# Where scores, value products and transposes stand in PE's order: slots 5 to 17 and the first batch of an attention and bilinear FFN kernel

## The chip, the cores and the metric

One core of a Trainium2 chip. Times are device microseconds of one execution. The profile's span starts a little later and ends a little earlier: an execution of 415.64 us has a span of 413.9.

## The reference

```python
scores = scale * q @ k.T                      # 8 batches, 8 heads, 576 x 576, head size 64
scores += bias_table[bucket(|i - j|)]         # relative position bias
attn = softmax(scores)                        # without a mask
x = (attn @ v) -> (4608, 512)                 # heads side by side
out = ((x @ w_a) * (x @ w_b)) @ w_out         # 512 -> 1536 -> 512
```

## The kernel before

Two heads make a pair; the 32 pairs are worked on in 32 slots. In slot s, PE computes the scores of pair s and the value products of pair s - 1, and the FFN's matmuls of finished batches fill the rest. ACT takes exponentials from PSUM, DVE multiplies by exp(bias) (`mul`) and normalises (`norm`). 576 is 4 x 128 + 64, so each pair has "tail" scores and a 64-column corner, `qktt`.

```python
def qk_tail(p):                               # tail scores of pair p
    ps = ps_sc.tile(...)
    ...
    pt = bank(AV if wide(p) else TR, FP32, f"qktt{p}")     # the corner's own bank
    ...
def ex_tail(p):                               # ACT: L395 reads the corner, then L397 or L400 the rest
```

PSUM has two banks for FFN units (FF, used in turn) and one each called AV and TR. AV holds value products 0 to 2 of a pair, TR products 3 and 4, and both also take transposes, corner scores and, in `run`, one FFN unit each. `run(s, four)` interleaves the four score tiles of slots from 9 on with four half-row FFN units; between two halves a 1x1 copy on DVE (`hop`) must have run. After it:

```python
first = o[0:1] or rest[0:1]                   # an output unit, or, where the plan has none, an input unit
rest = rest if o else rest[1:]
steps += [lambda: run(s, four), lambda: qk_tail(s), lambda: put_in(first, FF), lambda: ex_tail(s),
          lambda: mul(s, 0)] + TQ + X(o[1:2]) + [lambda: mul(s, 1)]
steps += TK + X(o[2:]) if o else []
steps += [A(0, 1, 2), N(0)]                   # value products 0 to 2, norm
steps += [] if o else TK
steps += X(rest[0:1]) + [lambda: mul(s, 2), A(3, 4), N(3), lambda: t_x(s - 1), lambda: turns(s)]
...
```

`TQ` and `TK` are PE's transposes of the next pair's queries and keys with their copies (slots up to 10); `t_x` and `turns` issue transposing DMAs from the SP queue: the attention output of the pair before, and from batch 3 on the queries, keys and tails of the next batch.

The softmax here doesn't subtract the row's maximum and nothing guards it: scores larger than these inputs give would overflow.

## Time and profile before

| | before |
|---|---|
| time, median of 4 | 414.91 us (414.62 to 414.97) |
| PE busy share, DVE, ACT | 96%, 49%, 59% |
| slot 11 and slot 17, score start to score start | 8.30 and 9.16 us |
| a usual slot (19 to 30) | 10.79 us |

PE is the bound almost everywhere, so a slot's length, read from the timeline as the start of one slot's first score matmul to that of the next, shows at once what a wait costs. The prediction shows the lines that matter (its list of PE's waits is a choice: the page also has 1.2 us before the first scores and a few of 0.2 to 0.7 us).

### The profile page before, as it was taken

To read this page: it belongs to the slowest core of one execution; us is meant where nothing else is said; L and a number is where in the kernel's file an instruction comes from. 1 tells how busy PE (TensorE), PEld (TensorE's weight loads), DVE (VectorE), ACT (ScalarE), POOL (GpSimd) and SP (SyncE) were. 2 spreads that over 40 slices of the span, in tenths; PEclk is the share of its full clock that TensorE was granted. 3 is DMA by queue.
4 is the path that set the end of the run, shared out by engine and by line. 5 is a ranking of instruction groups with operands and counts; after the bars stand their busy time and mean duration, and the time that the engine had idled before them with its cause. 6 is when DMAs were issued, how large, how long until landed. Compare 5 with 4: busy or idle time off the path is not lost.

```text
span 413.9 us, 9454 instructions
## 1 busy us (share of the span) xinstructions
PE 399.2 (96%) x3831; PEld 218.9 (53%) x3890; DVE 201.0 (49%) x531; ACT 244.0 (59%) x345; POOL 119.6 (29%) x161
## 2 busy tenths in 40 slices
PE   8799999999999999999999999999999999999996
PEld 3574555566656555555555555555555544444443
DVE  4685666656465444644455455555544330430330
ACT  4997476676887666766666666666666222322321
POOL 9897848904455006600550030000000000000000
PEclk9999999999999999999999999999999999999999
DMA  9999999999979939992899249421111202002004
GB/s 159 189 155 178 158 159 150 180 147 125 140 54 169 164 47 85 152 143 63 78 170 145 64 61 122 92 65 42 35 35 41 65 2 102 2 0 102 2 1 101
DMA packets 164940, 40.83 MB, mean 99 GB/s; under 512 B 155320, under 2 KB 160224, under 8 KB 164896
## 3 DMA queue, kind: packets, MB, share of 16 engines
q0 software_dynamic: 110448, 18.75, 63.9%
q1 hardware_dynamic: 53168, 21.03, 27.7%
q8 instruction: 30, 0.49, 0.5%
q10 hardware_dynamic: 1280, 0.43, 0.5%
q14 instruction: 14, 0.11, 0.1%
HBM read 38.77 MB, written 9.45 MB: 116 GB/s over the span
## 4 chain that ended last, share of the span: by engine, by line
PE 82%; DMA 10%; POOL 4%; issue 2%; DVE 1%; ACT 1%; POOLq 0%; DVEq 0%
PE pa L538 21%; PE po L538 21%; PE pb L538 20%; PE av L432 7%; PE qk L347 6%; DMA wb<-in_moe_w_b_dram 4%; DMA kn<-in_k_dram 4%; PE av L423 2%; DMA vm<-in_v_dram 2%; PE qkt L378 2%; PE qkt L375 1%; PE po L555 1%; POOL qn L134 1%; POOL kn L134 1%; DVE XG L469 1%
## 5 line engine op out<-in xcount | busy, mean ns | idle before, releaser
L538 PE MATMUL pb<-xn,wb 64*128 64x512 bf16 (+1 forms) x592 | 156.6, 377 | 1.3
L538 PE MATMUL pa<-xn,wa 128*128 128x512 bf16 (+1 forms) x609 | 157.2, 377 | 0.7 <-DVE XG L469 0.3
L358 ACT ACTIVATE at<-qk 128x1024 bf16<-128x1024 f32 x128 | 129.3, 1026 | 38.6 <-PE qk L347 36.3
L544 ACT ACTIVATE ha<-pa 128x512 f32<-128x512 f32 x108 | 64.8, 600 | 61.8 <-PE pa L538 60.7
L538 PEld LDWEIGHTS <-wa 64*128 64x128 bf16 (+1 forms) x616 | 56.6, 96 | 44.3 <-DVE XG L469 2.3
L538 PEld LDWEIGHTS <-wb 64*128 64x128 bf16 (+1 forms) x616 | 56.8, 96 | 41.1 <-issue 1.5
L548 DVE TENSOR_TENSOR g<-pb,ha 128x512 bf16<-128x512 f32 x60 | 41.5, 692 | 65.5 <-PE pb L538 38.3
L366 DVE TENSOR_TENSOR at<-at,W 128x512 bf16<-128x512 bf16 (+1 forms) x128 | 59.4, 483 | 2.3 <-DMA W<-bias_tab 2.1
L128 POOL DMA_DIRECT2D vm<-in_v_dram x32 | 28.2, 918 | 95.1 <-PE av L432 83.5
L573 ACT ACTIVATE ob<-po 128x512 f32<-128x512 f32 x35 | 20.9, 598 | 55.6 <-PE po L538 53.6
L538 PE MATMUL po<-wo,g 128*128 128x512 bf16 x216 | 51.8, 379 | 0.6
L432 PEld LDWEIGHTS <-at 128*128 128x128 bf16 x992 | 39.3, 97 | 8.7 <-issue 3.3
L432 PE MATMUL av<-vm,at 128*128 128x65 bf16 x992 | 42.9, 193 | 0.0
L548 DVE TENSOR_TENSOR q<-pb,ha 128x512 bf16<-128x512 f32 x32 | 22.1, 692 | 41.8 <-ACT ha L544 21.0
L423 PE MATMUL av<-vt,att 128*128 128x130 bf16 x156 | 34.6, 222 | 2.3 <-ACT att L395 2.2
L538 PEld LDWEIGHTS <-g 128*128 128x128 bf16 x228 | 21.5, 98 | 22.9 <-issue 0.7
L468 DVE RECIPROCAL rc<-av 128x6 f32<-128x6 f32 x64 | 12.1, 188 | 44.1 <-PE av L432 43.5
L469 DVE TENSOR_TENSOR XG<-av,rc 128x384 bf16<-128x384 f32 x64 | 31.4, 491 | 2.2
L347 PE MATMUL qk<-QTb,KTb 64*128 64x512 bf16 x160 | 32.0, 379 | 0.0
L128 POOL DMA_DIRECT2D qn<-in_q_dram x28 | 24.3, 911 | 21.7 <-PE trq L296 14.3
L538 PE MATMUL po<-wo,q 128*128 128x512 bf16 x116 | 29.6, 379 | 0.6
L128 POOL DMA_DIRECT2D kn<-in_k_dram x28 | 24.4, 914 | 3.4 <-DMA wb<-in_moe_w_b_dram 1.8
(133 smaller groups left out, 349.2 us busy)
## 6 DMA issues: line engine op xcount, KB each, us to landing
out_dram<-ob SPq DMA_DIRECT2D x32, 256.0 KB, 2.3
vm<-in_v_dram POOLq DMA_DIRECT2D x28, 128.0 KB, 5.5
qn<-in_q_dram POOLq DMA_DIRECT2D x24, 128.0 KB, 8.0
kn<-in_k_dram POOLq DMA_DIRECT2D x24, 128.0 KB, 8.3
wa<-in_moe_w_a_dram POOLq DMA_DIRECT2D x3, 512.0 KB, 7.4
wb<-in_moe_w_b_dram POOLq DMA_DIRECT2D x3, 512.0 KB, 9.5
wo<-in_moe_w_out_dram POOLq DMA_DIRECT2D x1, 1536.0 KB, 13.3
W<-bias_tab POOLq DMA_DIRECT2D x4, 192.0 KB, 5.6
```

The source lines that it names most:

```text
L128: nc.gpsimd.dma_start(out=(vm[b % 2][:, h0:h1, t, 0:Dh] if dst is None else dst[b % 2][:, :].rearrange("p (t h d) -> p t h d", h=H, t=NM)[ ...
L347: nc.tensor.matmul(out=ps[:, hh, :], lhsT=kT_(p, t)[r, :], rhs=qT[r, :, :], start=True, stop=True)
L358: nc.scalar.activation(out=at[:, :, :], in_=ps[:, :, :], func=ACTF.Exp, scale=scale)
L366: nc.vector.tensor_tensor(out=at[:, :, lo:hi], in0=at[:, :, lo:hi], in1=w[:, :, y:(None if z < 0 else z):-1], op=MULT)
L423: nc.tensor.matmul(out=pav[:, slot, :, :], lhsT=x, rhs=vt[b // 2 % 2][:, 4 * i + hp, :, 0:Dh + 1], start=fresh, stop=True, skip_group_chec ...
L432: nc.tensor.matmul(out=pav[:, slot, hh, :], lhsT=x, rhs=vm[i][:, 2 * hp + hh, t, 0:Dh + 1], start=False, stop=True, skip_group_check=True)
L468: nc.vector.reciprocal(out=rc, in_=pav[:, 0:n, :, Dh])
L469: nc.vector.tensor_tensor(out=xg[:, j0:j0 + n, :, :], in0=pav[:, 0:n, :, 0:Dh], in1=rc.unsqueeze(3).to_broadcast([128, n, 2, Dh]), op=MULT)
L538: return nc.tensor.matmul(out=o[:, :], lhsT=w[r, :], rhs=m[r, :], start=first if start is None else start, stop=final if stop is None else ...
L544: nc.scalar.activation(out=ha[:, :], in_=ff.pop(("pa", df))[:, :], func=ACTF.Copy)
L548: nc.vector.tensor_tensor(out=g_sb[c % 2][df][:, :], in0=ff.pop(("pb", df))[:, :], in1=ff.pop(("ha", df))[:, :], op=MULT)
L573: nc.scalar.activation(out=ob[:, :], in_=po[:, :], func=ACTF.Copy)
```

## The change

Its intent is to remove PE's waits. In slots without output units (10, 11, 12, 17) corner scores move from AV to an FF bank, and the value products come straight behind. In slots 5 to 8 key transposes move behind the tail scores; in slot 8 the output transposes move as well. In the first batch two score tiles of pair 1 go ahead of tail scores, and pair 2's copies ahead of the bias products on DVE.

```diff
-    def qk_tail(p):
+    def qk_tail(p, where=TR):
...
+        pt = bank(where, FP32, f"qktt{p}")
...                                            # first batch, cut
+    qk1(1, 0)
     tails_next(0, 2, None)
...
+    qk1(1, 1)
+    ex(1, 1)
+    qk_tail(0, AV)
...
+        if s == 1:
+            q_next(1)
+            k_next(1)
+            mul(0, 0)
...                                            # slots from 9 on
+            back = [lambda: norm(s - 1, 3), lambda: t_x(s - 1), lambda: turns(s)]
+            if o:
...                                            # the old order
+            else:
+                steps += [lambda: qk_tail(s, FF), lambda: ex_tail(s), A(0, 1, 2), N(0), lambda: mul(s, 0)] + TQ
+                early_x = X(rest[0:1]) + TK + X(rest[1:2])
+                steps += (early_x if e else []) + [lambda: mul(s, 1), A(3, 4)] + back + [lambda: mul(s, 2)]
+                steps += ([] if e else early_x) + [lambda: mul(s, 3), lambda: mul_tail(s)]
...                                            # slots 5 to 8
-                      lambda: ex(s, 3), U, lambda: mul(s, 2), lambda: t_k(s + 1, AV), lambda: c_k(s + 1),
-                      U, lambda: mul(s, 3), lambda: qk_tail(s), lambda: ex_tail(s), U]
+                      lambda: ex(s, 3), U, lambda: mul(s, 2)]
+            steps += X1 if s == R4 - 1 else []
+            steps += [U, lambda: mul(s, 3), lambda: qk_tail(s), lambda: ex_tail(s),
+                      lambda: t_k(s + 1, AV), lambda: c_k(s + 1), U]
```

## The prediction

> **What bounds the kernel now.** I read the page first. PE is busy for 96% of the span at a full granted clock, and the chain of waits is 82% PE; the only other large share is 10% DMA.
>
> ```profile
> PE 399.2 (96%) x3831; PEld 218.9 (53%) x3890; DVE 201.0 (49%) x531; ACT 244.0 (59%) x345; POOL 119.6 (29%) x161
> PE 82%; DMA 10%; POOL 4%; issue 2%; DVE 1%; ACT 1%; POOLq 0%; DVEq 0%
> ```
>
> The change adds and removes no matmul, so it can only remove holes in PE. The span less PE's busy time is 413.9 - 399.2 = 14.7 us, of which about 5 us before the first scores and the tail after 410 us are not touched. A gain of 2% is 8.3 us, so it would have to take nearly everything left. Busy time also hides some loss: a record lasts 379 ns, but in the timeline four 512-column matmuls start within 0.86 us, 0.216 us each. I therefore measure a hole from where the next start was due, not from the "idle" figure.
>
> Next, PE's own waits, longest first:
>
> ```profile
> PE av L423 <- ACT att L395: 2.2, 3, 0.8
> PE trx L495 <- DVE XG L469: 0.7, 3, 0.3
> PE trk L316 <- DMA kn<-in_k_dram: 0.6, 1, 0.6
> PE qktt L388 <- DVE QT L262: 0.6, 1, 0.6
> PE pa L538 <- DVE XG L469: 0.3, 1, 0.3
> ```
>
> Three value products wait for ACT. They are exactly slots 10, 11 and 17, where the plan gives no output units. PE and ACT in slot 17 (start, us, engine, line, x count):
>
> ```profile
> 164.61 0.22 PE L388 MATMUL qktt<-QTt,KTt 128*128 128x64 bf16 x2
> 164.72 1.02 PE L538 MATMUL pa<-xn,wa 128*128 128x512 bf16 x3
> 166.54 0.22 PE L423 MATMUL av<-vt,att 128*128 128x130 bf16 x1 [0.80 <-ACT att L395]
> ...
> 165.78 0.60 ACT L544 ACTIVATE ha<-pa 128x512 f32<-128x512 f32 x1 [0.43 <-PE pa L538]
> 166.27 0.22 ACT L395 ACTIVATE att<-qktt 128x64 bf16<-128x64 f32 x1
> ```
>
> The corner scores qktt sit in the AV bank. Value products need that bank, ACT must read it first (L395), but ACT's order puts the copy of pa ahead, and pa ends on PE only at 165.6. So PE waits for ACT, which waited for PE. The products were due at 164.72 + 4 x 0.216 = 165.58 and began at 166.54: **0.96 us lost**. In the same way slot 11 lost 108.56 - 107.60 = 0.96 and slot 10 lost 98.76 - 98.02 = 0.74. Slot 12 also has no outputs, but its first unit is a pb, which gives ACT nothing to do, and it has no wait.
>
> The earlier part is tied to transfers. In slot 7 the last transpose of pair 8's keys waits for its load, with the tail scores of slot 7 still behind it in PE's order:
>
> ```profile
> 71.01 0.38 PE L316 MATMUL trk<-cst_sb,kn 128*128 128x128 bf16 x3
> 72.01 0.23 PE L316 MATMUL trk<-cst_sb,kn 128*128 128x128 bf16 x1 [0.62 <-DMA kn<-in_k_dram]
> 72.19 0.39 PE L381 MATMUL qkt<-KT 128*128 128x128 bf16 x4
> ```
>
> ```profile
> 50.09 1.03 POOL L168 DMA_DIRECT2D wo<-in_moe_w_out_dram  x1
> ...
> 63.94 0.89 POOL L128 DMA_DIRECT2D qn<-in_q_dram  x1 [7.45 <-PE qktt L388]
> 64.81 3.51 POOL L128 DMA_DIRECT2D kn<-in_k_dram  x4
> ```
>
> The page puts the stall of the load queue at 63.94 down to PE. I do not believe it: just ahead of that load the trace has a semaphore instruction at 63.43 on the semaphore that the output weights' load counts up, and that load took 13.3 us from issue to landing, 50.09 + 13.3 = 63.4. So the keys land at 71.96 whatever PE does before.
>
> **What the Trainium skill says.** (1) "PSUM — Partial Sum Buffer", section "Engine vs sequencer instructions": ScalarE and VectorE are strict FIFO and matmuls start in program order. The 165.78/166.27 pair agrees: a finished qktt waited behind a copy of a later matmul's result. (2) Same page, "PSUM bank collisions raise a hardware error": guard by bank, not by address. That is why 64 columns of corner scores hold up value products; the 0.96 us agrees. (3) "Perfetto Trace Analysis", section "Identifying Dependency Chains": an instruction with several waits may have EventSemaphore instructions ahead of it. The one at 63.43 is of that kind and is my ground against the page's releaser. (4) "VectorE: DVE Perf Modes", the section on the TRN2 errata, gives a matmul max(60, 6 + columns) cycles at 2.4 GHz, 0.216 us for 512; the trace's 0.86 us for four agrees.
>
> **The change part by part.** Each step keeps before's times and shifts what moves.
>
> *First batch.* Pair 1's first two tiles go ahead of the tails, so ACT no longer stands 0.41 us before 12.25. Pair 2's copies no longer queue behind the bias products, which wait for the bias table until 14.75 on DVE, so qktt of slot 1 does not wait 0.57 us at 17.14. Value products of pair 0 still need the bias products, about 2 us of DVE after 14.75, and could start near 16.8 instead of 17.25. I put the lead at 0.4 to 0.65 us by 19 us. It is **worth 0** at the end: slot 7's keys land at 71.96 and the lead becomes a longer wait.
>
> *Slots 5 to 7.* The key transposes move behind the tail scores (in slot 5 behind a unit too, which covers a short wait for keys at 52.1). In slot 7 the tail scores, 72.19 to 72.68, now run while PE would have waited: **0.49 us**, the only part of the early stage that survives.
>
> *Slot 8.* Pair 7's output transposes move from in front of the third score tile to behind pair 9's query transposes and a unit. Before, PE lost 77.70 to 78.16 there for the norm, and about 0.25 more up to 79.23 for the copy out of that bank. All 0.7 go. New: qktt in that bank now comes right after trx and must wait for the copy of 0.52 us on DVE, which I put at 0.3 to 0.35 us. Net **0.35 us**.
>
> *Slot 10.* Corner scores go to an FFN bank, value products right behind them; 0.74 us and the 0.31 us before 101.16 go. Against it: qktt waits about 0.15 us for the product out of its bank (96.19 to 96.88 on DVE); the pa unit waits 0.15 us for the next; and key transposes follow query transposes by one unit in one bank, with DVE now doing the norm (0.70 us) and a bias product (0.33) before the copy (0.42), so PE waits about 0.5 us. Net **0.2 us**.
>
> *Slots 11 and 17.* The same swap without transposes. AV is free (its copy ended at 163.94), TR is free at 165.35, when the last two products want it at 165.73; the FFN units then find their banks free. Each gets 0.96 back less about 0.08 for qktt's wait: **0.88 us each, 1.76**.
>
> *Slot 12.* No wait to remove, but its norm moves ahead of two bias products, so slot 13's half-row unit in AV need not wait at 118.50 (due 117.80; slot 13's score part took 4.82 us against 4.32 in slot 11). That is 0.5 us, less about 0.2, because DVE's queue still reaches slot 13's small sync copy only near 120.0, and PE would want it at 119.95. **0.3 us**.
>
> Slots 9, 13 to 16 and from 18 on keep their order. Sum: 0.49 + 0.35 + 0.2 + 1.76 + 0.3 = 3.1 us; 414.95 - 3.1 = **411.85 us**.
>
> **The rivals.** *The early lead survives*: if the page is right that PE released the load at 63.94, keys land earlier with PE, and up to 1 us more is won, 411 us. The semaphore at 63.43 speaks against it. *The wait only moves*: ACT still has the same queue, and TR's earlier user leaves at 165.35, only 0.4 us before it is wanted; a slow norm on DVE could delay the small sync copies of the next half-row part. If slots 10 to 12 give nothing, 0.9 us for slot 17 and 0.8 for slots 7 and 8 remain: 413.2. *DVE becomes the bound in slots 8 to 13*: it carries 49% over all, but with the norm ahead of the copies the transposes of slot 10 wait; doubled, this loses another 0.6. *ACT is the true limit*: against it, ACT idles 2.03 us after slot 17's tails, so work pulled forward finds it free.
>
> **Range and chances.** The well-measured terms (slots 11, 17 and 7) make 2.25 us; the rest, 0.85, could be zero or double, and the early lead could add 1. So 410.7 to 413.3, with repeats within 0.35 us. Neither 2% edge is near: faster 0.01, same 0.98, slower 0.01.
>
> **What would show it.** PE's waits for ACT att L395 gone; slot 17 near 8.25 us instead of 9.16, slot 11 near 7.4 instead of 8.30; a new short wait of qktt for a copy in slot 8 and of key transposes for DVE in slot 10; the keys of pair 8 still landing near 72.0, with PE's wait for them no shorter than 0.35 us although tail scores now stand ahead of it. I am wrong if that landing moves with PE, or if slot 11 or 17 keeps its length.

## The result, and the profile after

412.70 us, median of 4 (412.48 to 413.23), against 414.91 us. The ratio is 0.995, 95% interval 0.9933 to 0.9967; ratios here are the mean time of one kernel's fast runs over that of the other's of the same rounds, so not quite the ratio of the medians. The time lies in the stated range, but the gain is 2.2 us and not 3.1. Of the page after, PE's busy line, then the chain that ended last by engine:

```profile
PE 397.7 (97%) x3831; PEld 216.3 (53%) x3890; DVE 201.0 (49%) x531; ACT 243.8 (59%) x345; POOL 119.5 (29%) x161
PE 86%; DMA 4%; POOL 3%; DVE 3%; issue 1%; SPq 1%; ACT 1%; POOLq 0%; ACTq 0%; DVEq 0%
```

The DMA share of the chain fell from 10% to 4%, and a new entry of SP's queue came in. PE's waits in the changed kernel (total us, times, longest), the first four and one more:

```profile
PE warm L217 <- DVE zero_sb L194: 1.2, 1, 1.2
PE qkt L378 <- DMA KTt<-ktl: 1.1, 1, 1.1
PE trx L495 <- DVE XG L469: 0.7, 3, 0.3
PE trk L316 <- DVE QT L262: 0.6, 1, 0.6
...
PE pb L538 <- DVE k L548: 0.4, 1, 0.4
```

All three waits of value products for ACT are gone. Three of those shown are new: tail scores that wait for a DMA, KTt; key transposes that wait for a copy on DVE; and, in slot 13, an FFN unit that waits for DVE's product (L548) of an earlier unit. Slot 17 after, PE and then ACT:

```profile
162.43 0.22 PE L388 MATMUL qktt<-QTt,KTt 128*128 128x64 bf16 x2
162.53 0.22 PE L423 MATMUL av<-vt,att 128*128 128x130 bf16 x1
...
162.92 0.26 ACT L395 ACTIVATE att<-qktt 128x64 bf16<-128x64 f32 x1
```

The products start 0.10 us behind the corner scores and before ACT has touched them; the FF bank took ACT off PE's path. Slot 12 after, on PE, and the SP queue ahead of it:

```profile
111.23 0.28 PE L375 MATMUL qkt<-QTt,KTb 64*128 64x64 bf16 x8
112.63 0.39 PE L378 MATMUL qkt<-QTb,KTt 128*128 128x256 bf16 x2 [1.12 <-DMA KTt<-ktl]
```

```profile
100.72 1.19 SPq L484 DMA_TRANSPOSE xn<-XG  x1
101.96 1.22 SPq L487 DMA_TRANSPOSE xn<-XG  x1
103.27 1.23 SPq L331 DMA_TRANSPOSE QTt<-qtl  x1
104.56 1.30 SPq L331 DMA_TRANSPOSE KTt<-ktl  x1
```

KTt, the transposed tail keys of batch 3, is issued fourth in a row, behind two transposes that wait for slot 10's norm (it ends at 100.69). It took 8.0 us to land, at 112.6, and PE lost 1.1 us. In the kernel before, the same transpose and the same tail scores stood like this:

```profile
106.71 1.37 SPq L331 DMA_TRANSPOSE KTt<-ktl  x1
114.83 0.39 PE L378 MATMUL qkt<-QTb,KTt 128*128 128x256 bf16 x2
```

There PE came 8.12 us after the issue, and KTt had landed after 6.16, at 112.86. In the changed kernel PE comes 6.95 us after the issue.

Slot by slot, from the timelines of the two profiles:

| slot | before | after | change | predicted |
|---|---|---|---|---|
| start of slot 5 | 45.74 | 44.80 | -0.94 | counted 0 |
| 5 | 10.44 | 10.17 | -0.27 | counted 0 |
| 7 | 8.43 | 7.73 | -0.70 | -0.49 |
| 8 | 8.20 | 7.93 | -0.27 | -0.35 |
| 10 | 9.97 | 9.71 | -0.26 | -0.2 |
| 11 | 8.30 | 7.50 | -0.80 | -0.88 |
| 12 | 7.41 | 8.47 | **+1.06** | 0 |
| 13 | 9.77 | 9.67 | -0.10 | -0.3 |
| 17 | 9.16 | 8.31 | -0.85 | -0.88 |

The changes, with 0.04 from slot 18, sum to 3.17, the whole difference of the spans (413.9 - 410.7). Yet the timed difference is 2.2: the profiled execution of the kernel before took 415.64 us, slower than its timed ones, that of the changed kernel was its fastest, 412.48. So some entry above varies from one execution to the next; the experiments had to say which.

### The profile page after: what moved, and what is told of

It reads as the page before. It is cut to its first block, busy times and chain, and to the rows that moved or that the text cites. A ratio compares the mean times of both kernels' runs of the same rounds, so it can differ in the third digit from the quotient of the medians.

```text
span 410.7 us, 9455 instructions
## 1 busy us (share of the span) xinstructions
PE 397.7 (97%) x3831; PEld 216.3 (53%) x3890; DVE 201.0 (49%) x531; ACT 243.8 (59%) x345; POOL 119.5 (29%) x161
## 4 chain that ended last, share of the span: by engine, by line
PE 86%; DMA 4%; POOL 3%; DVE 3%; issue 1%; SPq 1%; ACT 1%; POOLq 0%; ACTq 0%; DVEq 0%
PE po L538 22%; PE pa L538 21%; PE pb L538 21%; PE av L432 8%; PE qk L347 6%; DMA KTt<-ktl 2%; PE av L423 2%; PE qkt L378 2%; DMA W<-bias_tab 2%; DVE XG L469 1%; DVE at L366 1%; POOL vm L128 1%; PE po L555 1%; PE qkt L375 1%; PE trx L495 1%
## 5 line engine op out<-in xcount | busy, mean ns | idle before, releaser
L548 DVE TENSOR_TENSOR g<-pb,ha 128x512 bf16<-128x512 f32 x60 | 41.5, 692 | 64.8 <-PE pb L538 37.8
L548 DVE TENSOR_TENSOR q<-pb,ha 128x512 bf16<-128x512 f32 x32 | 22.1, 692 | 42.1 <-PE pb L538 21.2
L347 PE MATMUL qk<-QTb,KTb 64*128 64x512 bf16 x160 | 31.0, 379 | 0.0
```

What stands on the lines that cost most here:

```text
L347: nc.tensor.matmul(out=ps[:, hh, :], lhsT=kT_(p, t)[r, :], rhs=qT[r, :, :], start=True, stop=True)
L548: nc.vector.tensor_tensor(out=g_sb[c % 2][df][:, :], in0=ff.pop(("pb", df))[:, :], in1=ff.pop(("ha", df))[:, :], op=MULT)
```

## The experiments

All results matched the reference unless told otherwise. My theory (theory A in the expectations): the slots' waits are as the prediction had them, the loads of the first 72 us swallow the early lead, and a wait for KTt, made by PE's own lead, took about 1 us back. Rivals: the first batch's order brings the loads themselves earlier (theory B; keys of pair 8 landed at 70.55 us in the changed kernel's profile, at 71.96 before; a landing here is the last of 16 counts on the load's semaphore in the trace), or they vary by chance (theory C).

### Each part alone

**First batch alone**: the first batch's lines of the diff; `qk_tail` takes a bank but keeps its old one everywhere else.

> The kernel before with the new order of the first batch alone. Theory A (the prediction: the keys of pair 8 land at a time that PE does not set): the time stays within 0.3 us of before, 414.6 to 415.2 us; PE is 0.6 to 0.9 us earlier at slot 5 and waits that much longer in slot 7; the last load of pair 8's keys lands at 71.7 to 72.2 us. Theory B (the new order of the first batch makes the loads themselves come earlier, as the changed kernel's profile has them, at 70.5): 413.3 to 414.0 us, landing near 70.5.

Measured: 415.07 us, ratio 1.000 (0.9985 to 1.0015). Its one profile had keys at 70.65, as theory B has it, but that execution took 414.31 us, and none of the six (414.27 to 416.1) came down to B's 413.3 to 414.0.

**Slots 5 to 8 alone**: the last hunk.

> The kernel before with the new order of slots 5 to 8 alone. Both theories: 0.85 us less (0.5 from the tail scores of slot 7 run during the wait for keys, 0.35 from slot 8), 413.8 to 414.3 us. Theory A: keys land at 71.7 to 72.2. If the keys land at 70.5 here as well, although the first batch is untouched, the landing varies from run to run (theory C) and then the time would be near 413.

Measured: 414.45 us, ratio 0.9989 (0.9972 to 1.0006), so 0.45 us with 0.7 either way, which tells it apart neither from 0 nor from 0.85. Slot 8 was 7.93 us, as in the changed kernel, and slot 7 was 7.61: no wait, with keys at 71.42. Slot 12, which this edit does not touch, was 7.59 instead of 7.41: its KTt took 8.26 us to land and came too late by a little even with the old slots.

**Slots 10, 11, 12 and 17 alone**: the hunk of slots from 9 on.

> The kernel before with the new order of slots 10, 11, 12 and 17 alone (corner scores in an FFN bank, value products right behind). By the prediction 2.26 us less, 412.65 us, with slot 11 and slot 17 0.9 us shorter each. If the wait for the transposed tail keys that the changed kernel shows in slot 12 (1.1 us) comes from PE's own lead in slots 10 and 11, it shows here too, at 0 to 1 us, and the time is 412.7 to 413.6.

Measured: 414.11 us, ratio 0.9974 (0.9962 to 0.9986): 1.1 us and not 2.26. Slots 10, 11 and 17 were 9.72, 7.50 and 8.31, as after; slot 12 was 8.06 instead of 7.41, with this wait:

```profile
PE qkt L378 <- DMA KTt<-ktl: 0.7, 1, 0.7
```

So this part brings the wait for KTt without any help of the early ones.

**First batch and slots 5 to 8 together**: all but slots 10 to 17.

> The kernel before with the first batch and slots 5 to 8 in the new order, slots 10 to 17 as before. Theory A (keys land at their own time, and PE's lead of the first batch becomes a wait): no faster than slots 5 to 8 alone, ratio to before 0.9985 to 0.999, some 414.4 us. Theory B (the loads come earlier with the first batch's order, and the lead lives): 0.9 us below slots 5 to 8 alone, 413.2 to 413.7 us, slot 7 at 7.6 to 7.75 us, keys landing at 70.5 to 70.8 us.

Measured: 414.34 us, ratio 0.9981 (0.9967 to 0.9996), by the ratio between the two theories' figures and within noise of slots 5 to 8 alone. Its one profile looked as B has it: keys at 70.15, slot 7 at 7.61. The gains add up: 0.19% here and 0.26% for the other slots make 0.45%, against 0.5% for the whole change. Of the 0.84 us forecast for the early part some 0.8 came by this ratio, of the 2.26 for the other slots 1.1, each with about 0.6 us either way: the shortfall lies mostly in the latter.

### The wait for the tail keys

**Tails turned first**: in the changed kernel, slot 10 alone.

```diff
-            back = [lambda: norm(s - 1, 3), lambda: t_x(s - 1), lambda: turns(s)]
+            back = [lambda: norm(s - 1, 3)] + ([lambda: turns(s), lambda: t_x(s - 1)] if s == 10 else
+                                               [lambda: t_x(s - 1), lambda: turns(s)])
```

> The changed kernel with one edit: in slot 10 the transposing DMAs of the tail queries and keys are issued ahead of those of the attention output. If the 1.1 us of PE in slot 12 is a wait for the tail keys' transpose behind other transposes and loads, it goes, slot 12 is 7.4 us again instead of 8.5, and the time is 411.4 to 412.0 us. Rival: the load burst for batch 4 holds up every transpose alike, or the delayed output transposes are waited for instead: 412.4 to 412.9 us.

Measured: 411.81 us, ratio 0.9921 (0.9909 to 0.9933). Slot 12 is 7.29 us. The SP queue and PE:

```profile
96.48 1.96 SPq L331 DMA_TRANSPOSE QTt<-qtl  x1
98.49 1.27 SPq L331 DMA_TRANSPOSE KTt<-ktl  x1
101.01 1.20 SPq L484 DMA_TRANSPOSE xn<-XG  x1
...
111.53 0.28 PE L375 MATMUL qkt<-QTt,KTb 64*128 64x64 bf16 x8
111.74 0.39 PE L378 MATMUL qkt<-QTb,KTt 128*128 128x256 bf16 x2
```

In SP's order the tails' transposes no longer stand behind a transpose that waits for slot 10's norm, so they start at 96.48 instead of 103.27, and KTt lands at 104.9, 7 us before PE asks. The output's transposes are hardly later (101.01 against 100.72). Where the changed kernel in its two sets has a ratio of 0.995, this has 0.992: the wait cost some 1.1 us.

**Control**: the same edit in the kernel before.

> Control: the kernel before with the tails' transposes issued first in slot 10, nothing else. It has no wait for them, so 0.0 plus or minus 0.3 us; if it is faster by more, the 1 us that this edit gave in the changed kernel was not that wait.

Measured: 414.91 us, ratio 1.0003 (0.9984 to 1.0021). Slot 12 kept its 7.41 us. The edit alone gives nothing that the interval (0.7 us less to 0.9 more) shows; it gives some 1.1 us only where the new order has put PE ahead of the landing.

### Chance or order: the early landings

**The changed kernel again**, unedited.

> The changed kernel once more, unedited, for a comparison on one chip: 412.5 to 413.2 us, slot 12 at 8.0 to 8.5 us with the wait for the transposed tail keys. If the landing of pair 8's keys varies by chance (theory C) it may be anywhere from 70.5 to 72.4 us in the profile; if the first batch's order moves it (theory B) it is 70.5 to 70.8 again.

Measured: 413.12 us, ratio 0.995 (0.9936 to 0.9964). Keys landed at 71.61 this time, slot 7 took 8.23 us, slot 12 8.28. PE's waits for loads:

```profile
PE qkt L378 <- DMA KTt<-ktl: 0.9, 1, 0.9
PE av L423 <- DMA vt<-in_v_dram: 0.9, 1, 0.9
...
PE trk L316 <- DMA kn<-in_k_dram: 0.4, 1, 0.4
```

The early lead had already been lost in part in slot 1, to the load of the tail values, and in part in slot 7.

**The kernel before again**, one look.

> The kernel before, unedited, one profile more. Theory B: keys of pair 8 land at 71.4 to 72.4 us, as in the three profiles with the old first batch. Theory C (chance): anywhere from 70.5 to 72.4. Slot lengths other than slot 7 the same to 0.05 us.

Measured: 414.91 us, keys at 71.22, slot 7 at 8.11, the slots that PE alone sets unchanged to 0.02 us. So the start of slot 5, slot 5 (10.18 against 10.44) and slot 7 are what varies from execution to execution.

Over all profiles the keys landed at 70.6 to 72.5 us with the old first batch (six, mean 71.7) and at 70.1 to 71.7 with the new (eight, mean 70.8); slot 5 began at 45.6 to 46.0 (mean 45.77) and at 44.5 to 46.6 (mean 45.30). Theory B is refuted in its strict form, since 71.61 and 71.65 occur with the new order. The ranges overlap, but the means are 0.9 us apart, so that the order moves the mean landing is not excluded; if it does, the way is not known.

**Without the wait for pair 8's keys.** I wanted slot 7 free of its load, and let pair 8's key transposes read pair 4's buffer.

```diff
-            nc.tensor.transpose(..., blocks(kn, p)[:, t, :, :], ident)
+            nc.tensor.transpose(..., blocks(kn, 4 if p == 8 else p)[:, t, :, :], ident)
```

> The kernel before, but the key transposes of pair 8 read keys that landed long ago (wrong result on purpose for that pair), so that slot 7 cannot wait for pair 8's keys. Slot 7 is 7.6 us instead of 8.1 to 8.8, everything behind unchanged: 0.5 to 0.9 us less, 414.0 to 414.5 us.

Measured: 428.64 us, ratio 1.0336. The edit was a mistake: by slot 7 the load of batch 3's keys into that same buffer is already in order, so the transposes waited for it, far longer than for their own:

```profile
PE trk L316 <- DMA kn<-in_k_dram: 10.6, 4, 9.3
```

(The output still passed the comparison, though pair 8 read wrong keys; the check is not sharp enough for one pair.)

**The same with the new first batch.**

> The same, with the first batch in the new order (wrong result on purpose). Theory A (the lead of the first batch is real, some 0.5 us by slot 5, and is eaten only by the wait for keys): 0.4 to 0.9 us below the run without the wait and with the old first batch, 413.2 to 413.9 us. Rival (the lead is an accident of the profiled executions, or is lost to other loads earlier): within 0.2 us of that run.

Measured: 428.40 us, ratio 1.0322 (1.0303 to 1.0341), the same as without the new first batch (1.0317 to 1.0354). The two answer the question in another way than planned. PE came to slot 7 at 65.18 us with the old first batch and at 64.19 with the new, and to slot 8 at 85.68 and 85.97. Where a load is late enough, a lead of 0.99 us at slot 7 is worth nothing at slot 8. Its wait:

```profile
PE trk L316 <- DMA kn<-in_k_dram: 11.6, 4, 10.4
```

It is 1.0 us longer, just the lead. What the first batch is worth where no load is late was not measured; that stays open.

### Versions that beat both kernels

**Query copy first**: with the tails turned first, slot 10's copy of the queries goes ahead of norm and bias product on DVE.

```diff
-                steps += [lambda: qk_tail(s, FF), lambda: ex_tail(s), A(0, 1, 2), N(0), lambda: mul(s, 0)] + TQ
+                steps += [lambda: qk_tail(s, FF), lambda: ex_tail(s), A(0, 1, 2)] + TQ + [N(0), lambda: mul(s, 0)]
```

> The changed kernel with the tails turned first and, in slot 10, the query transposes and their copy ahead of the norm and the bias product on DVE. The 0.56 us that PE waits for this copy before the key transposes goes: slot 10 from 9.71 to about 9.15 us, 411.2 to 411.5 us in all. Rival: the norm, now later, is waited for by the next slot's half-row unit, or the load burst of batch 4 is waited for instead: 411.7 us or more.

Measured: 411.28 us, ratio 0.9920 (0.9902 to 0.9937). Slot 10 fell from 9.72 to 9.11 us: 0.6 us, as expected. The two ratios, 0.9921 without it and 0.9920 with it, come from two sets of runs and show no gain; a gain of 0.6 us lies within their intervals.

**Bias product before the norm** in slots 11, 12 and 17, on top.

```diff
-A(0, 1, 2)] + TQ + [N(0), lambda: mul(s, 0)]
+A(0, 1, 2)] + TQ + ([N(0), lambda: mul(s, 0)] if e else [lambda: mul(s, 0), N(0)])
```

> The best version so far (tails turned first, query copy first) with DVE's first bias product ahead of the norm in slots 11, 12 and 17. In slot 12 DVE stands still before the norm; filled with the product (0.33 us), its queue reaches slot 13's small sync copy 0.3 us earlier, and PE's wait of 0.43 us there falls to 0.1: slot 13 from 9.67 to 9.35 us, 410.9 to 411.2 us. Rival: DVE was not idle there once the transposed tail keys are early, and nothing moves: 411.3 us.

Measured: 411.08 us (410.07 to 411.9), ratio 0.9907 (0.9888 to 0.9925). Slot 13 fell from 9.67 to 9.33 us. In slot 12 of this version DVE now works while it waits for the products (it stood idle for 0.62 us there in the version without this edit):

```profile
113.08 0.41 DVE L366 TENSOR_TENSOR at<-at,W 128x512 bf16<-128x512 bf16 x1
113.78 0.20 DVE L468 RECIPROCAL rc<-av 128x6 f32<-128x6 f32 x1 [0.29 <-PE av L432]
```

This is the best version, some 0.4% below the changed kernel by the two ratios, which come from two sets of runs.

## Why the prediction was right or wrong

The time fell into the range, with the largest terms right, one step wrong, and some luck. The prediction's own terms span 410.0 to 412.7 us (2.25 us sure, 0.85 that could be zero or double, 1 for the early lead); the stated 413.3 leaves room for the rival "the wait only moves". In part that rival came true, in a slot and by a DMA that it did not name.

*Slots 11 and 17* (0.88 each): **right**, 0.80 and 0.85, by the mechanism named: PE had waited for ACT, which had waited for PE. (The records of pa end at 165.74, not at 165.6; nothing rests on it.)

*Slot 10* (0.2): **right**, 0.26, and its new wait for the copy on DVE was 0.56, forecast at 0.5.

*Slot 8* (0.35): **right** in kind; 0.27. The new wait for the copy was 0.18, not 0.3 to 0.35.

*Slots 5 to 7* (0.49 surviving): **right** in mechanism. Slot 7 took 8.02 to 8.79 us in its old order and 7.61 to 8.23 in its new one in the profiles of unharmed kernels, and 7.61 is its length without a wait. Where the keys landed equally late in the slot (6.15 us after its start in the second profile of the kernel before, 6.12 in slots 5 to 8 alone), it was 8.11 and 7.61: 0.50 us.

*The first batch worth 0 because the keys land at 71.96 "whatever PE does before"*: the result held (ratio 1.000), the fixed time did not. I took one landing for a constant; it ranges over 2.4 us, and in the profile of the changed kernel my own sign (keys near 72.0, a wait of at least 0.35 us) failed: they landed at 70.55, with no wait listed. That the forecast 0 held is partly luck. In an execution with early keys, such as the profiled one of the changed kernel, the lead of 0.94 us lives; in others it is eaten, in slot 1 or in slot 7. The rival that PE releases the loads is refuted. In all 14 profiles this load starts 0.53 us after the output weights' load lands, whatever the profile names as releaser, and the changed kernel's own profile names the load that I took from the semaphore:

```profile
61.40 0.89 POOL L128 DMA_DIRECT2D qn<-in_q_dram  x1 [6.60 <-DMA wo<-in_moe_w_out_dram]
```

*"Slot 12. No wait to remove", with 0.3 us gained in slot 13*: **wrong**, and the source of the missing 0.9 us. I asked which waits the new order removes and whether PE, ACT and DVE could follow, but not which transfers had been just in time. In the kernel before, KTt landed at 112.86 and PE asked at 114.83, 2 us later, in that one profile; in the second profile of the same kernel it landed at 113.72, 0.35 us before PE asked. Slots 10 and 11, shorter by a microsecond together, used that up: they cut the time from KTt's issue to its use from 8.12 us to 6.95, while its landing took 5.95 to 8.26 us over the 14 profiles. Slot 12 grew by 0.65 to 1.06 us in every version with the new slots and the old SP order, where the landing took 7.6 to 8.0, and turning the tails first gave it back. Slot 13's own term was also mis-sized, and its wait misplaced: PE waited 0.43 us, not 0.2, and by the profile not for the small sync copy but for DVE's product ahead of it in the same queue, so 0.10 was left:

```profile
117.28 0.37 PE L538 MATMUL pb<-xn,wb 64*128 64x512 bf16 x1 [0.43 <-DVE k L548]
```

With slot 12's loss at the 0.9 to 1.06 of the changed kernel's two profiles and slot 13 at 0.1, the forecast sum of 3.1 becomes 1.8 to 2.0; measured, 2.2.

## What to carry to other kernels

When work on the bound engine moves forward, list the transfers that it will now meet earlier, with the slack of each, and take the slack from several executions: an order of DMAs that was good enough can become the next wait. The wait on a shared bank went when its small user got another bank (0.8 us in each of slots 11 and 17), and the queue order of a third engine shows who really waits for whom. Value a lead ahead of a late load at nothing, and look at what else could be done during that wait instead.

## What the Trainium skill lacked or had wrong

- "DMA: Bandwidth & Descriptors", section "Issuing engines are not separate DMA queues", says that DMAs of all issuing engines share the same 16 DMA engines and interleave. The runs are in line with it: batch 3's KTt transpose from SP, issued while POOL's loads for batch 4 were on their way, took 5.95 to 8.26 us to land in the 14 profiles, and later ones 2.4 us at best. The page gives no such landing time for a transpose under load.
- No page says how far landings vary between executions of one program: the keys' landing, some 70 us into the run, ranged from 70.6 to 72.5 us in six profiles with the same first batch.
- "Perfetto Trace Analysis", section "Identifying Dependency Chains", mentions waits put in separate EventSemaphore instructions; it does not warn that a profile which names one releaser beside the instruction can then name a wrong one. Here PE was named for a 7.45 us wait that the semaphore instruction at 63.43 us ties to a load, which landed at 63.41.
- Nothing on the pages that the prediction names was found wrong; the matmul cost of 0.216 us for 512 columns that it takes from there holds in its trace.
